# Second layer pair by pair, tiles turned in place, and h and u kept in DRAM tile by tile

## The chip, the cores and the metric

The kernel runs on one core of one Trainium2 chip. The metric is the device time of one execution in microseconds (us). The time outside the profile's span is the execution's own time less the span from its first to its last instruction.

## What is computed

All arrays are float32. The core of the reference:

```python
# attention: batch 4, 12 heads, 448 positions, head size 64
scores = q @ k.T / sqrt(64) - log(448)
x = (sigmoid(scores) @ v), heads side by side           # 1792 x 768
# layer one
h = maximum(maximum(x @ w1, x @ w2), x @ w3)             # 1792 x 768
y = h @ w_out                                            # 768 x 768
# layer two
h = y @ w_in                                             # 1792 x 1024
e = exp(h - max(h))
solu = h * e / sum(e)
ln = (solu - mean(solu)) / sqrt(var(solu) + 1e-6) * g_ln
out = ln @ w_out2                                        # 1024 x 768
```

## The kernel before

**Arithmetic.** Float32 operands are split into a high part and a rest, and each product is three matmuls (high x high, high x rest, rest x high). Layer one and layer two use a Strassen-Winograd scheme: a 2 x 2 block product is seven products P1 to P7 (table `PROD`), on sums and differences of blocks. An operand of a product needs a copy by ScalarE (the high part), a subtraction by VectorE (the rest), and for four of the seven a sum first.

**Stages.** Attention comes first, with the weight conversions between its halves. There the product w_out @ w_in is formed, so that layer two's first half, L, is one product of h with a 768 x 1024 weight. Then layer one runs over 9 column groups times two halves of the batch (`units`). Each unit opens P1, closes P4 and P3 of the unit before, and does P2, P6, P5 and P7. When a block of h is done, `sums` writes it to DRAM (`h_d`). Layer two follows: 14 tiles of 128 rows, taken as seven pairs, first L for all pairs, then O (the product with the last weight). The list `tiles` puts tiles 7 to 13 first, so pair 0 is tiles 7 and 8.

**L and O.** `groups` gives the order: L takes pairs 0 and 1 together, then 2, 3 and 4 alone, then 5 and 6 together; O takes 0 and 1 together and then the others alone. A group opens P1 of its first pair (`begin`), closes P4 and P3 of the group before (`fourth`, `third`), and does P2, P6, P5, P7 (`second`, `sixth`, `fifth`, `seventh`). After P1, P6 and P7 ScalarE copies the PSUM tile X, and the next product of X waits for that copy. An L product is 9 matmuls of 512 columns, an O product 12 of 384. The seven weights of L are loaded by GpSimd (`load_wf`) at the end of layer one; `hold` is a small copy on GpSimd by which its queue waits for a tile. While the last pair of L goes through its products, each product's weight slot is given to a weight of O (`release`, `load_w2`).

**Normalization.** After a pair's P3, `solu_ln` is appended to the queue `lazy`. It is a chain of ScalarE and VectorE steps over two tiles: exponential, product, square, a few small steps on sums, scaling; then VectorE turns 32 x 32 blocks (`dve.transpose`) into an `e` tile and SP writes it to DRAM (`u_d`). `load_u(p)` reads a pair's turned tiles back for O. Its `while` loop writes out steps of the queues until the pair's tiles, and for p > 0 the second tile of pair p + 1, are turned.

**Order.** The queues of TensorE, ScalarE, VectorE and (from the end of layer one) GpSimd run in the order in which the program writes their instructions. Each matmul of layer two adds 0.227 (L) or 0.174 (O) to a budget (`pace`), and steps of `bg` (operands: `prep_l`, `prep_o`) and then of `lazy` are written as long as it is above zero, each taking its cost off. An L pair's operands cost 6.26 together, an O pair's 7.69, a chain of `solu_ln` 6.74, an L sum 0.78, an O sum 0.56. A product whose operand is not yet written out takes steps of `bg` whatever the budget (`product_c`). Operands stand in a ring of 10 slots, one for an L operand and two for an O operand. `load_h` brings a pair's tiles of h from DRAM (`next_h` in layer two).

**Buffers.** L's results and the turned tiles read back share the tag `hu`, 10 buffers (pair 0 has two of its own); `e` has 3.

Of the kernel before, what the change touches and what calls it, by code (L numbers as in the profile page):

```python
# [44 lines left out]
def sigmoid_attention_max_moe_solu_ln(tc, q, k, v, w123, wo, wi, w2, g, out):  # L45
# [56 lines left out]
    h_d = {(k, bp): dram.tile([3, P, 2 * S], F32, name=f"h_d{k}{bp}") for k in range(2) for bp in range(2)}  # L102
# [548 lines left out]
    def sums(u, i, j, ps, add):  # L651
# [20 lines left out]
        if w == 2:  # L672
            sp.dma_start(out=h_d[i, bp][fp, :, j * S : (j + 1) * S], in_=h)
# [26 lines left out]
    def load_h(p, k, rows=slice(0, 3)):  # L700

        for i in range(2):
            bp, c0 = divmod(tiles[2 * p + i] * P, 2 * S)
            sp.dma_start(
                out=h_tile(p, i, k)[:, rows], in_=h_d[k, bp][rows, :, c0 : c0 + P].rearrange("f p t -> p f t")
            )
# [154 lines left out]
    for n, u in enumerate(units):  # L861
# [8 lines left out]
        if old is not None:  # L870
# [4 lines left out]
            if old["u"] == (NG - 1, 1):  # L875
# [7 lines left out]
                for k in range(2):  # L883
                    hold(hts[(1, 1, k)][:, :8])
# [7 lines left out]
        if n == len(units) - 1:  # L892
            bg.append(in_turn(prep_l(0), prep_l(1), 8))
# [5 lines left out]
        if u == (NG - 1, 1):  # L899
# [3 lines left out]
            af_cm, afirst = open_pool("afirst", 1)  # L903
            load_h(0, 0, slice(0, 2))
# [4 lines left out]
            for tag in (0, 1):  # L909
                load_wf(LOADS[tag], tag)  # L910
# [67 lines left out]
    def solu_ln(p):  # L978
# [4 lines left out]
        for i, t in enumerate(pair):  # L983
            e.append(tp.tile([P, 2, 512], F32, tag="e", name=f"e{t}", bufs=3))
# [29 lines left out]
        for i, t in enumerate(pair):  # L1014
            ub = e[i].rearrange("p a b -> p (a b)")
            dve.transpose(out=ub, in_=h[i].rearrange("p a b -> p (a b)"))
            sp.dma_start(out=u_d[t].rearrange("i f r e -> (i f) (r e)"), in_=ub)
            turned.add(t)
            yield 1.25

    def load_u(p):
        for t in tiles[2 * p : 2 * p + 2]:
            while t not in turned or (p + 1 < NP2 and tiles[2 * p + 3] not in turned and p > 0):
                step(bg)
                assert step(lazy), t
            ut = (hfirst if p == 0 else tp).tile([P, 4, 256], F32, tag="hu", name=f"ut{t}", bufs=2 if p == 0 else 10)
            for r in range(4):
                sp.dma_start(out=ut[r * 32 : (r + 1) * 32], in_=u_d[t][:, :, r].rearrange("i f e -> f i e"))
# [28 lines left out]
    def targets(kind, p):  # L1057
# [4 lines left out]
        for t in tiles[2 * p : 2 * p + 2]:  # L1062
            h = (hfirst if p == 0 else tp).tile([P, 2, 512], F32, tag="hu", name=f"h{t}", bufs=2 if p == 0 else 10)
# [98 lines left out]
    groups = [("L", g) for g in ((0, 1), (2,), (3,), (4,), (5, 6))]  # L1162
    groups += [("O", g) for g in ((0, 1), (2,), (3,), (4,), (5,), (6,))]
# [122 lines left out]
```

## Time and profile before

| | |
|---|---|
| median of 3 runs | 701.18 us (698.69 to 705.81) |
| profiled execution, its own time | 700.64 us |
| its span | 698.9 us |
| TensorE busy in the span | 651.9 us, 93% |
| VectorE busy | 490.7 us, 70% |
| ScalarE busy | 372.4 us, 53% |
| mean granted TensorE clock | 0.977 of full speed |

Busy time of TensorE comes from modelled, overlapping matmuls, so a busy TensorE is not one at its peak. A granted clock of 1.00 is 2.4 GHz; the lower level is 1.2 GHz. In the timelines a bracket at the end of a line is the idle time of that engine before the line, and what ended it. Names leave buffer numbers out: `XL` is the PSUM tile X in L, `XO` in O, `c_L_A` and `c_O_S` are operands, `wfB`/`wfT` and `w2tB`/`w2tT` weights, `a` the tiles of h, `ut` the turned tiles.

### The profile page before, as it was taken

The numbers are of one execution on the slowest core, as the hardware profiler recorded it, in microseconds if no ns is written. First come the engines' busy times: TensorE is split into PE (matmuls) and PEld (weight loads), VectorE is DVE, ScalarE is ACT, GpSimd is POOL, SyncE is SP. The second block draws the span as 40 slices with busy tenths as digits, with TensorE's granted clock in tenths as the row PEclk, the third lists the DMA queues.
The fourth block names the chain that finished last, engine by engine and source line by source line (L and its number), as shares of the span: only waits on it lengthen the run. The fifth ranks groups of instructions, "written<-read, shape, count | busy, mean of one in ns | idle before, by whom it ended". The sixth has DMA issues, their size and how long they took to land.

```text
span 698.9 us, 9717 instructions
## 1 busy us (share of the span) xinstructions
PE 651.9 (93%) x3283; PEld 526.4 (75%) x3283; DVE 490.7 (70%) x1070; ACT 372.4 (53%) x712; POOL 72.4 (10%) x149
## 2 busy tenths in 40 slices
PE   9999999999999999999999998899997887786797
PEld 6555688545569999999999997678875786776697
DVE  4799987797458788868977875447885674645552
ACT  5888433678665554554455443235766354635241
POOL 1111110001000111011011001210013500000000
PEclk9999999999999999999999999999999799988999
DMA  8788678736301565654674439992539956362211
GB/s 295 216 257 248 191 270 307 282 122 206 117 1 28 158 193 187 185 153 149 179 218 149 117 110 315 318 364 79 159 91 312 303 167 166 80 181 102 74 46 68
DMA packets 82977, 125.16 MB, mean 179 GB/s; under 512 B 35568, under 2 KB 62704, under 8 KB 82928
## 3 DMA queue, kind: packets, MB, share of 16 engines
q1 hardware_dynamic: 71344, 70.84, 32.5%
q0 software_dynamic: 11440, 53.48, 24.1%
q8 instruction: 26, 0.43, 0.3%
q10 hardware_dynamic: 144, 0.23, 0.1%
q14 instruction: 23, 0.19, 0.1%
HBM read 84.15 MB, written 40.37 MB: 178 GB/s over the span
## 4 chain that ended last, share of the span: by engine, by line
PE 56%; DVE 21%; DMA 8%; ACT 8%; issue 6%; SPq 1%; POOL 0%; DVEq 0%; ACTq 0%; POOLq 0%
PE x L643 18%; PE v L643 9%; PE XO L948 6%; PE z L643 4%; PE av L272 4%; PE XL L948 3%; PE VO L948 3%; PE sc L251 3%; DMA ut<-u_d 2%; PE ZO L948 2%; DMA a<-h_d 2%; ACT e L996 2%; DMA wfT<-w_dT 1%; DVE y_wi L157 1%; ACT h L1012 1%
## 5 line engine op out<-in xcount | busy, mean ns | idle before, releaser
L272 PE MATMUL av<-sf,vr 128*64 128x448 f32 x384 | 77.5, 546 | 0.0
L259 ACT ACTIVATE sf<-sc,bias_s 128x896 f32<-128x896 f32 x72 | 67.6, 1009 | 1.3
L141 POOL DMA_DIRECT2D raw<-in_w x52 | 28.2, 542 | 279.7 <-DVE S L56 140.0
L272 PEld LDWEIGHTS av<-sf,vr 128*64 128x64 f32 x384 | 25.4, 137 | 40.8 <-issue 35.7
L251 PE MATMUL sc<-qt,kt 64*128 64x448 f32 x432 | 52.0, 377 | 3.2 <-ACT sf L256 3.2
L472 PE MATMUL pw<-wi_t,r_wo 128*128 128x512 f32 x216 | 49.6, 391 | 0.0
L251 PEld LDWEIGHTS sc<-qt,kt 64*128 64x128 f32 x432 | 38.2, 185 | 15.1 <-issue 5.9
L472 PEld LDWEIGHTS pw<-wi_t,r_wo 128*128 128x128 f32 x216 | 40.4, 188 | 9.4 <-issue 1.0
L683 ACT COPY u<-x 128x448 f32<-128x448 f32 x36 | 19.1, 530 | 43.2 <-PE x L643 43.2
L948 PE MATMUL XO<-w2tT,c_O_S 128*128 128x384 f32 x168 | 32.4, 340 | 6.6 <-ACT c_O_S L51 6.2
L948 PE MATMUL XL<-wfT,c_L_S 128*128 128x512 f32 x126 | 32.4, 409 | 4.0 <-DMA wfT<-w_dT 3.0
L948 PEld LDWEIGHTS XO<-w2tT,c_O_S 128*128 128x128 f32 x168 | 29.0, 188 | 8.5 <-ACT c_O_S L51 7.2
L643 PE MATMUL x<-T3h,S 128*128 128x448 f32 x108 | 33.7, 366 | 0.0
L643 PE MATMUL x<-B11h,A 128*128 128x448 f32 x108 | 33.7, 366 | 0.0
L643 PE MATMUL x<-T4h,A 128*128 128x448 f32 x108 | 33.6, 365 | 0.0
L643 PE MATMUL x<-T2h,S 128*128 128x448 f32 x108 | 33.6, 365 | 0.0
L643 PE MATMUL v<-B22h,S 128*128 128x448 f32 x108 | 33.6, 365 | 0.0
L643 PE MATMUL z<-B21h,A 128*128 128x448 f32 x108 | 33.6, 365 | 0.0
L643 PE MATMUL v<-T1h,S 128*128 128x448 f32 x108 | 33.6, 365 | 0.0
L948 PEld LDWEIGHTS XL<-wfT,c_L_S 128*128 128x128 f32 x126 | 24.6, 197 | 10.6 <-issue 3.8
L412 ACT ACTIVATE raw<-raw,g_sb 128x192 f32<-128x192 f32 x32 | 13.3, 466 | 31.3 <-DVE raw L157 31.3
L157 DVE SCALAR_TENSOR_TENSOR raw<-raw 128x384 int32<-128x384 int32 x52 | 29.0, 557 | 1.1
(185 smaller groups left out, 1561.6 us busy)
## 6 DMA issues: line engine op xcount, KB each, us to landing
raw<-in_w POOLq DMA_DIRECT2D x52, 384.0 KB, 4.1
w_d<-w2s SPq DMA_DIRECT2D x48, 192.0 KB, 2.4
u_d<-e SPq DMA_DIRECT2D x14, 512.0 KB, 3.0
ut<-u_d SPq DMA_DIRECT2D x56, 128.0 KB, 3.9
kr<-in_k SPq DMA_DIRECT2D x24, 256.0 KB, 3.4
vr<-in_v SPq DMA_DIRECT2D x24, 256.0 KB, 4.0
raw<-in_wi POOLq DMA_DIRECT2D x16, 384.0 KB, 4.5
w_dT<-wsT SPq DMA_DIRECT2D x12, 512.0 KB, 3.5
```

The lines of the kernel that those rows point to most:

```text
L141: pool.dma_start(out=t, in_=source(key).rearrange("p (n t) -> p n t", t=2))
L157: dve.scalar_tensor_tensor(out=yi, in0=raws[key][:, cols, 0], scalar=29, in1=yi, op0=ALU.logical_shift_right, op1=ALU.bitwise_or)
L251: pe.matmul(sc[:, j, :S], lhsT=kt[rows, x, c * P : (c + 1) * P], rhs=qt[rows, y], start=start, stop=stop)
L259: act.activation(sf, sc[:, :, :S], AF.Sigmoid, bias=bias_s, scale=1.0 / math.sqrt(D))
L272: pe.matmul(pa[j * D : (j + 1) * D, :S], lhsT=vr[:, j, c], rhs=sf if c == 3 else sf[:, j], start=(n == 0), stop=(n == 3),)
L412: act.activation(half, half, AF.Copy, scale=g_sb[:, kc + 4 * i : kc + 4 * i + 1])
L472: pe.matmul(ps, lhsT=wt[:, a, cols], rhs=wi_t[:, b, c0 : c0 + 512], start=(i == 0), stop=(i == 3 * KC - 1))
L643: pe.matmul(ps, lhsT=l, rhs=r, start=(start and c == 0 and i == 0), stop=(stop and c == 2 and i == 2), skip_group_check=True)
L683: act.copy(e, ps)
L948: pe.matmul(ps, lhsT=hl[l][:, c * P : (c + 1) * P], rhs=wt[:, c, m], start=(start and c == 0 and i == 0), stop=(stop and c == chunks - 1 a ...
L996: act.activation(e[i], h[i], AF.Square, bias=su[:, c], scale=-float(F2), accum_out=vs[:, c])
L1012: act.activation(h[i], h[i], AF.Identity, bias=nb[:, c], scale=s1[:, c])
```

## The change

- The turn writes back into the h tile (`h[i]`), and the write to DRAM reads from there. `e` has 2 buffers instead of 3, `hu` 11 instead of 10.
- `u_d` is laid out so that a tile is read back by one DMA of whole rows; it is written by four DMAs, one for every 32 partitions, in pieces of 256 words.
- `load_u` waits for its own pair's tiles alone.
- L takes its seven pairs one by one; O is grouped as before. `load_u(2)` and `load_u(3)` come one step later in O's first group, and `next_h(p + 2)` follows P6 of pair p throughout.
- `h_d` holds tiles of 128 rows of h whole, so that `load_h` reads rows of 256 or 384 words in one piece; `sums` writes each block in two DMAs, one with three tiles' columns (128 each) and one with the 64 columns of the tile that two blocks share.
- The first weight of L is asked for before pair 0's tiles of h; the `hold` for pair 1's tiles is gone. Pair 1's operands are queued in pair 0's L group instead of in turn with pair 0's.

```diff
--- before.py
+++ after.py
@@ -99,7 +99,7 @@
 
     w_d = {nm: dram.tile([P, 3, 2 * 512 + 16], F32, name=f"w_d{nm}") for nm in LOADS}
     w2_d = [dram.tile([4, P, len(nms), 2, HU], F32, name=f"w2_d{n}") for n, nms in enumerate(PIECES)]
-    h_d = {(k, bp): dram.tile([3, P, 2 * S], F32, name=f"h_d{k}{bp}") for k in range(2) for bp in range(2)}
+    h_d = {(k, bp): dram.tile([TT // 2, P, 3, P], F32, name=f"h_d{k}{bp}") for k in range(2) for bp in range(2)}
     u_d = [dram.tile([4, 32, 4, 256], F32, name=f"u_d{t}") for t in range(TT)]
 
 
@@ -670,7 +670,12 @@
             tt(add, ps, add, ALU.add)
             tt(h, add, h, ALU.max)
         if w == 2:
-            sp.dma_start(out=h_d[i, bp][fp, :, j * S : (j + 1) * S], in_=h)
+            to, c = h_d[i, bp][:, :, fp], j * D
+            sp.dma_start(
+                out=to[4 * j : 4 * j + 3].rearrange("t p c -> p t c"),
+                in_=h[:, c : c + 3 * P].rearrange("p (t c) -> p t c", t=3),
+            )
+            sp.dma_start(out=to[3, :, c : c + D], in_=h[:, 3 * P * (1 - j) :][:, :D])
 
     def held(u, nm, ps):
         k = state["e"] % 5
@@ -700,10 +705,8 @@
     def load_h(p, k, rows=slice(0, 3)):
 
         for i in range(2):
-            bp, c0 = divmod(tiles[2 * p + i] * P, 2 * S)
-            sp.dma_start(
-                out=h_tile(p, i, k)[:, rows], in_=h_d[k, bp][rows, :, c0 : c0 + P].rearrange("f p t -> p f t")
-            )
+            bp, t = divmod(tiles[2 * p + i], TT // 2)
+            sp.dma_start(out=h_tile(p, i, k)[:, rows], in_=h_d[k, bp][t][:, rows])
 
     def last_rows(k):
 
@@ -880,8 +883,6 @@
                 last_rows(1)
                 for k in range(2):
                     load_h(1, k)
-                for k in range(2):
-                    hold(hts[(1, 1, k)][:, :8])
                 for tag in (2, 3, 4):
                     load_wf(LOADS[tag], tag)
         Z = ps_z.tile([P, 512], F32, tag="z", name=f"z{n}")[:, :S]
@@ -890,7 +891,7 @@
         product(X, u, "P6", False, False)
         u2 = held(u, "u2", X)
         if n == len(units) - 1:
-            bg.append(in_turn(prep_l(0), prep_l(1), 8))
+            bg.append(prep_l(0))
         V = ps_v.tile([P, 512], F32, tag="v", name=f"v{n}")[:, :S]
         product(V, u, "P5", True, False)
         product(X, u, "P7", False, False)
@@ -901,13 +902,13 @@
             shut(xd_cm)
             wslot.update(weight_slots("sa", (0, 1)))
             af_cm, afirst = open_pool("afirst", 1)
+            load_wf(LOADS[0], 0)
             load_h(0, 0, slice(0, 2))
             load_h(0, 1, slice(0, 2))
             for k in range(2):
                 hold(hts[(0, 1, k)][:, :8])
             last_rows(0)
-            for tag in (0, 1):
-                load_wf(LOADS[tag], tag)
+            load_wf(LOADS[1], 1)
         old = dict(u=u, X=X, V=V, u2=u2)
     assert not raws and state["load"] == len(stream)
 
@@ -981,7 +982,7 @@
         h = [h2s.pop(t) for t in pair]
         e = []
         for i, t in enumerate(pair):
-            e.append(tp.tile([P, 2, 512], F32, tag="e", name=f"e{t}", bufs=3))
+            e.append(tp.tile([P, 2, 512], F32, tag="e", name=f"e{t}", bufs=2))
             c = slice(i, i + 1)
             act.activation(e[i], h[i], AF.Exp, bias=low[:, c], scale=-1.0, accum_out=ssum[:, c])
             yield 0.05
@@ -1012,20 +1013,23 @@
             act.activation(h[i], h[i], AF.Identity, bias=nb[:, c], scale=s1[:, c])
             yield 0.05
         for i, t in enumerate(pair):
-            ub = e[i].rearrange("p a b -> p (a b)")
-            dve.transpose(out=ub, in_=h[i].rearrange("p a b -> p (a b)"))
-            sp.dma_start(out=u_d[t].rearrange("i f r e -> (i f) (r e)"), in_=ub)
+            ub = h[i].rearrange("p a b -> p (a b)")
+            dve.transpose(out=ub, in_=ub)
+            for r in range(4):
+                sp.dma_start(
+                    out=u_d[t][:, :, r].rearrange("b f e -> f b e"),
+                    in_=ub[r * 32 : (r + 1) * 32].rearrange("f (b e) -> f b e", b=4),
+                )
             turned.add(t)
             yield 1.25
 
     def load_u(p):
         for t in tiles[2 * p : 2 * p + 2]:
-            while t not in turned or (p + 1 < NP2 and tiles[2 * p + 3] not in turned and p > 0):
+            while t not in turned:
                 step(bg)
                 assert step(lazy), t
-            ut = (hfirst if p == 0 else tp).tile([P, 4, 256], F32, tag="hu", name=f"ut{t}", bufs=2 if p == 0 else 10)
-            for r in range(4):
-                sp.dma_start(out=ut[r * 32 : (r + 1) * 32], in_=u_d[t][:, :, r].rearrange("i f e -> f i e"))
+            ut = (hfirst if p == 0 else tp).tile([P, 4, 256], F32, tag="hu", name=f"ut{t}", bufs=2 if p == 0 else 11)
+            sp.dma_start(out=ut, in_=u_d[t].rearrange("b f i e -> (b f) i e"))
             uts[t] = ut.rearrange("p i (k t) -> p k i t", k=K2)
 
     def prep_o(p):
@@ -1060,7 +1064,7 @@
             return [block(f"{nm}{p}") for nm in ("e1", "u2", "u3", "cx")]
         hh = []
         for t in tiles[2 * p : 2 * p + 2]:
-            h = (hfirst if p == 0 else tp).tile([P, 2, 512], F32, tag="hu", name=f"h{t}", bufs=2 if p == 0 else 10)
+            h = (hfirst if p == 0 else tp).tile([P, 2, 512], F32, tag="hu", name=f"h{t}", bufs=2 if p == 0 else 11)
             h2s[t] = h
             hh.append(h)
         return [hh[0][:, 0], hh[0][:, 1], hh[1][:, 1], hh[1][:, 0]]
@@ -1159,10 +1163,10 @@
         for k in range(2):
             load_h(p, k)
 
-    groups = [("L", g) for g in ((0, 1), (2,), (3,), (4,), (5, 6))]
-    groups += [("O", g) for g in ((0, 1), (2,), (3,), (4,), (5,), (6,))]
+    groups = [("L", (p,)) for p in range(NP2)] + [("O", g) for g in [(0, 1)] + [(p,) for p in range(2, NP2)]]
     prev = None
     for n, (kind, g) in enumerate(groups):
+        p, last = g[-1], n == len(groups) - 1
         if prev and len(prev) > 1:
             for o in prev:
                 fourth(o)
@@ -1184,40 +1188,31 @@
         now_open += [begin(kind, p) for p in g[1:]]
         if n == 2:
             load_w2(LOADS[0], 7)
-        if (kind, g) == ("L", (5, 6)):
+        if (kind, p) == ("L", NP2 - 1):
             load_u(1)
-        elif (kind, g) == ("O", (0, 1)):
-            load_u(2)
-        elif kind == "L" and 2 <= g[0] < 5:
-            next_h(g[0] + 1)
-        last = n == len(groups) - 1
         if not last:
             for o in now_open:
                 second(o)
+        if (kind, p) == ("O", 1):
+            load_u(2)
         for o in now_open:
             sixth(o)
-        if (kind, g) == ("L", (0, 1)):
-            next_h(2)
-        elif (kind, g) == ("L", (4,)):
-            next_h(6)
-            load_u(0)
-            bg.append(in_turn(prep_l(5), prep_l(6), 6))
-        elif kind == "L" and g[0] < 4:
-            bg.append(prep_l(g[0] + 1))
-        elif (kind, g) == ("L", (5, 6)):
-            bg.append(in_turn(prep_o(0), prep_o(1), 1))
+        if kind == "L":
+            if p + 2 < NP2:
+                next_h(p + 2)
+            if p == NP2 - 2:
+                load_u(0)
+            bg.append(prep_l(p + 1) if p + 1 < NP2 else in_turn(prep_o(0), prep_o(1), 1))
         elif not last:
-            bg.append(prep_o(g[-1] + 1))
-            if 2 <= g[0] < 5:
-                load_u(g[0] + 2)
+            bg.append(prep_o(p + 1))
+            if 1 < p < NP2 - 2:
+                load_u(p + 2)
         for o in now_open:
             fifth(o)
-        if (kind, g) == ("L", (0, 1)):
-            bg.append(prep_l(2))
-        elif (kind, g) == ("O", (0, 1)):
-            load_u(3)
         for o in now_open:
             seventh(o)
+        if (kind, p) == ("O", 1):
+            load_u(3)
         if last:
             for o in now_open:
                 second(o)
```

## Rows read from the trace of the kernel before

**Rows 1.** Page, part 2: TensorE busy share and granted clock.

```profile
PE   9999999999999999999999998899997887786797
...
PEclk9999999999999999999999999999999799988999
```

**Rows 2.** Stretches of layer two, cut between products: busy us per engine, clock, DMA.

```profile
429.50:472.80 43.30, 37.08 (x154) 29.75 (x154) 20.94 (x47) 14.99 (x29) 6.96 (x12) 0.96 0.94 342
472.80:487.30 14.50, 14.50 (x65) 11.87 (x64) 11.18 (x25) 8.54 (x19) 0.00 (x0) 1.00 0.29 83
...
517.70:555.00 37.30, 32.08 (x130) 25.83 (x128) 22.27 (x50) 19.47 (x39) 18.06 (x44) 0.91 0.87 275
555.00:596.20 41.20, 33.02 (x169) 30.45 (x170) 26.23 (x51) 20.39 (x38) 1.33 (x4) 0.96 0.60 174
596.20:617.80 21.60, 16.71 (x85) 16.39 (x84) 12.07 (x24) 13.06 (x24) 0.00 (x0) 0.84 0.46 135
617.80:644.10 26.30, 19.35 (x86) 17.27 (x86) 13.67 (x27) 13.14 (x25) 0.00 (x0) 0.87 0.39 113
644.10:668.00 23.90, 17.31 (x86) 15.72 (x85) 12.63 (x22) 7.11 (x15) 0.00 (x0) 0.93 0.27 74
668.00:682.60 14.60, 14.60 (x86) 14.60 (x85) 9.41 (x16) 6.37 (x13) 0.00 (x0) 1.00 0.14 54
```

**Rows 3.** Timeline of TensorE: start, length, work, idle before and its releaser.

```profile
429.30 0.37 PE L643 MATMUL x<-T3h,S 128*128 128x448 f32 x1
432.86 2.31 PE L948 MATMUL XL<-wfB,c_L_A 128*128 128x512 f32 x9 [3.19 <-DMA wfB<-w_dB]
...
541.60 7.14 PE L948 MATMUL XL<-wfT,c_L_A 128*128 128x512 f32 x18 [5.18 <-ACT h L1148]
...
550.68 4.28 PE L948 MATMUL VL<-wfB,c_L_S 128*128 128x512 f32 x18
...
611.63 4.21 PE L948 MATMUL XO<-w2tT,c_O_A 128*128 128x384 f32 x12 [4.89 <-ACT u L1148]
...
692.96 2.27 PE L948 MATMUL VO<-w2tB,c_O_S 128*128 128x384 f32 x12
```

**Rows 4.** Timeline of ScalarE around two late copies.

```profile
539.84 1.15 ACT L986 ACTIVATE e<-h,st 128x1024 f32<-128x1024 f32 x1 [5.18 <-DMA u_d<-e]
...
604.60 1.15 ACT L996 ACTIVATE e<-h,st 128x1024 f32<-128x1024 f32 x1 [0.81 <-DVE h L990]
...
608.85 2.37 ACT L1012 ACTIVATE h<-h,st 128x1024 f32<-128x1024 f32 x2 [1.02 <-DVE st L1008]
611.12 0.46 ACT L1148 COPY u<-XO 128x384 f32<-128x384 f32 x1
```

**Rows 5.** Timeline of GpSimd where the seven weights are asked for.

```profile
424.54 1.53 POOL L735 DMA_DIRECT2D wfB<-w_dB  x2 [0.66 <-DMA h_d<-hs]
...
439.28 0.58 POOL L731 COPY gate<-a 128x8 f32<-128x8 f32 x1 [1.88 <-DMA a<-h_d]
439.88 1.52 POOL L735 DMA_DIRECT2D wfT<-w_dT  x2
447.97 0.76 POOL L735 DMA_DIRECT2D wfT<-w_dT  x1 [6.57 <-issue]
```

**Rows 6.** Groups of VectorE instructions, layer two: busy us, mean ns, idle before.

```profile
L1016 DVE STREAM_TRANSPOSE e<-h 128x1024 f32<-128x1024 f32 x14 | 17.0, 1233 | 7.9 <-ACT h L1012 6.5 <-DMA u_d<-e 1.3
L990 DVE SCALAR_TENSOR_TENSOR h<-h,e 128x1024 f32<-128x1024 f32 x14 | 16.9, 1221 | 0.8 <-ACT e L986 0.8
```

**Rows 7.** DMA issues of the page, part 6: KB each, us to landing.

```profile
w_d<-w2s SPq DMA_DIRECT2D x48, 192.0 KB, 2.4
u_d<-e SPq DMA_DIRECT2D x14, 512.0 KB, 3.0
ut<-u_d SPq DMA_DIRECT2D x56, 128.0 KB, 3.9
```

**Rows 8.** DMA issues from 416 to 450 us, same columns.

```profile
a<-h_d SPq DMA_DIRECT2D x11, 192.0 KB, 10.1
```

## The prediction

> **What bounds the kernel now.** I read the busy shares in slices first, then a table of stretches, then the two timelines that explain the worst stretches. The slices show TensorE at nine tenths or more for the first two thirds of the span, and between six and nine tenths after that, with the granted clock at full speed nearly everywhere but in two later slices [rows 1]. So attention, the weight product and layer one leave nothing to win; layer two (L, then O) does. The stretches say how much. One L pair alone takes 14.5 us for seven products, 2.07 us each; one undisturbed O pair takes 14.6 us, 2.09 us each, both with TensorE busy throughout and the clock at 1.00 [rows 2]. Against these two prices I read three segments of the profiled execution (span 698.9 us, its own time 700.64 us, so 1.74 us lie outside the span; the median of the runs, 701.18, is the same within 0.1%):
> - Start: from the end of layer one's fifth product of the last unit, 429.7 us, to 472.8 us, 43.1 us for 15 L products and two leftovers of layer one. TensorE waits 3.19 us for the first weight, and later weights trail [rows 3, 5].
> - L: 472.8 to 555.0 us (end of the last V product of pairs 5 and 6), 82.2 us for 34 L products and one O product, which need 34 x 2.07 + 2.09 = 72.5. Excess 9.7 us. The table and the timeline put almost all of it late: a 5.18 us wait for a copy by ScalarE and 18 products behind it at the low clock, 7.14 us instead of 4.1 [rows 2, 3].
> - O: 555.0 to 695.2 us, 140.2 us for 48 O products, which need 48 x 2.09 = 100.3. Excess 39.9 us: four stretches of 41.2, 21.6, 26.3 and 23.9 us stand where 14, 7, 7 and 7 products need 29.3, 14.6, 14.6 and 14.6, so 11.9, 7.0, 11.7 and 9.3 us [rows 2]. The last two pairs have none.
>
> What ends those waits is not a busy engine: in the O stretches VectorE is busy 52 to 64% and ScalarE 30 to 61% [rows 2]. It is order. The load of a pair's turned tiles (load_u) may be written only when the *next* pair's second tile is turned, and until then it writes the next pair's whole normalization chain, at once, into the pinned queues of ScalarE and VectorE. Seen at pair 2 of O: the chain runs on ScalarE from the squares at 604.60 to the scaling that ends at 611.2, with pauses for VectorE inside; the copy that frees X stands behind it, at 611.12; TensorE waits 4.89 us for it and then does 12 matmuls in 4.21 us, the pace of the lower level of its clock, 1.2 instead of 2.4 GHz [rows 3, 4]. The forced chain also drives the budget below zero by its whole cost (6.74), so the next pair's operands come only when a product demands them: the excess goes on in the following stretches, the fourth of which holds no chain at all.
>
> **The change, part by part.**
>
> *Own pair alone (the condition in load_u), and single L pairs.* I follow the budget by hand. An L pair earns 63 x 0.227 = 14.3; its four sums take 3.1 and the next pair's operands 6.26, so 4.9 is left for a chain of 6.74. Chain 0 is ready at the end of pair 0, starts in pair 1, and with 4.9 a pair chains 0 to 3 are written out by pair 6's second product. From pair 6's fifth product to the sixth of O's pair 2, the place where pair 4 is asked for, 4 L products of 2.04 and 17 O products of 2.09 earn 43.7; sums take 6.2, the operands of O's pairs 0 and 1 15.4 and most of pair 2's about 7. Some 15 are left, or 2.2 chains: 4 and 5 are out when pair 4 is asked for, and 6 before pair 5 is. So no load forces a chain, and operands fall behind by one step (at most 1.32) instead of a whole chain. What remains are chains written at the budget's pace, of which O carries three (4, 5, 6) instead of about four. A pair with a chain fits: VectorE's 9.41 us plus (17.0 + 16.9) / 7 = 4.8 us, ScalarE's 6.37 us plus 6 calls, 7.0 us, each under 14.6 us [rows 2, 4, 6], though barely. A chain can still stand before a copy. The cost per chain is bounded by what the trace shows: nothing (the stretch 472.8 to 487.3 carries most of chain 0 and has no wait [rows 2]) and 7.0 us (the wait and the slow products above). I take 2 us each, near the lower end since the pace is that of the lower row, and 2 us for the doubled first group: O's excess 8 (3 to 25), a gain of 32. For L, 3 (1 to 8) instead of 9.7.
>
> *Turning in place, two e tiles, eleven hu tiles.* The turn itself keeps its 1.24 us [rows 6]. The wait that goes is the one in front of ScalarE's exponential at 539.84, 5.18 us for the write of an e tile still under way [rows 4]; that is the L wait named above, and its 6.7 us gain is counted there. What is late next: an hu tile. Eleven make the second turned tile of pair p take the place of the next pair's first h tile, so this load still waits for that tile's write. SP stands there, and behind it in its queue the output writes; nobody waits for either for a pair's time. I cost it at 0; without that cover it costs the write and load, 3.0 + 3.9 us, once a pair [rows 7].
>
> *Turned tiles written in four and read in one.* Both versions issue 14 x 5 DMAs; the write takes the form of the old reads (3.9 us), the read that of the old write (3.0 us) [rows 7]. Sum 0, and hidden, as each load has nearly a pair's lead.
>
> *h in DRAM by tiles.* 24 more small writes on SP, which is idle there, and loads of whole rows of 1,024 or 1,536 bytes instead of 512. Between 416 and 450 us such loads take 10.1 us beside the weights [rows 8]; the larger rows can only help. I cost it at 0 (0 to -2). The Trainium skill, "DMA: Bandwidth & Descriptors", section "Specifications", speaks against the 64-column rows: it says that writes under 512 bytes are done as read-modify-write. Here the w_d writes go in pieces of 96 columns, 384 bytes, and land in 2.4 us, sooner than the turned tiles' 1 KB pieces [rows 7]. If each new small write did cost such a time again, only the last before pair 1's load would count, and the sum would be 664 instead of 662.
>
> *Weights at the start.* The first is asked for when layer one has left its slot, at about 417 us instead of 424.5, and the gate that held the third until 439.9 is gone [rows 5]. But one pair now eats all seven weights. Seven times 1.57 MB (128 x 3 x 1,024 words), the tiles of pairs 0 to 2 (2.1 MB) and layer one's last h (1.4 MB) are 14.5 MB; at 342 to 400 GB/s, the first being the mean of that stretch [rows 2], 36 to 42 us from 417.5: the seventh lands at 454 to 460. It is needed by the last product of pair 0, and six more follow before the mark: 456 + 2.1 + 6 x 2.07 + some low clock = 472. The same as before: the 3.19 us won at the first weight are paid back at the fourth to seventh. I take 0, bounds -3 and +7 (the first weight no earlier than now).
>
> Sum: 700.6 + 0 - 6.7 - 32 = 662 us.
>
> **Rivals.**
> - *Chains go on costing.* Paced or not, a chain's 6.6 us on ScalarE stands before a copy that has one product of cover. If each of O's three still costs the 7.0 us of pair 2, O's excess is 23 with the first group's 2: 677. For it: both engines are then over 90% full. Against: chain 0's stretch.
> - *The change doesn't remove the wait.* Eleven tiles against twelve still tie pair p's load to pair p + 1's chain; if that holds back the operands as now, O's 39.9 stay and only L's 6.7 go: 694, no measurable change beside 700.6 (a difference under 1% can't be told from none in this kernel). Against: only ScalarE's and VectorE's written order made the wait, and the tile's turn is already in it.
> - *Slower.* Singles leave only one product, 2.07 us, between the third X copy and the product that needs X; in the old first and last groups there were two or more. If each of the seven chains is written just ahead of that copy, each costs what the pairs with 7.0 and 11.7 us lost, on average 9.4, so 66 us instead of the 9 in my sum (3 + 8, less the first group's 2): 662 + 57 = 719. It decides against the change once a chain costs over 7 us on average. Against: the L singles of now, with no wait between 472.8 and 487.3 [rows 2].
>
> **How the numbers follow.** Forecast 0.68, its own range 650 to 677 from start -3 to +7, L 1 to 5, O 3 to 14. Chains go on costing: 0.17. Wait not removed: 0.08. Slower: 0.07. Low end: 662 - 3 - 2 - 5 - 2 = 650. High end: into the first rival with the start's +7 and part of its O bound: 677 + 9 = 686. That leaves out the last two, 0.15. Faster by over 1% are the first two, 0.85; within 1% the third; slower the fourth.
>
> **What would show it.** Right: TensorE's waits for the third copies gone or under 2 us; no wait of the exponential for a DMA; four O stretches within 2 us of their products; all but three chains before O; the low clock in fewer slices. The start should show waits for the fourth to seventh weight. Wrong, if chains still run in unbroken blocks ahead of copies, if TensorE waits for operands in O as now, or if pair 1's operands wait for h tiles behind the weights.

## The result and the profile after

| | before | after |
|---|---|---|
| median of 4 runs each | 702.15 us (698.69 to 705.81) | 663.30 us (660.67 to 665.47) |
| ratio, 95% interval | | 0.944 (0.938 to 0.951) |
| profiled execution, its own time | 700.64 us | 665.47 us |
| its span | 698.9 us | 663.7 us |
| TensorE busy | 93% | 97% |
| mean granted TensorE clock | 0.977 | 0.994 |

The kernel is 5.6% faster; 662 us was forecast. In the slices of the page after (tenths of busy time; granted clock), the run of sevens and eights that ended the kernel before [rows 1] is gone, and what is left of it lies at the start of layer two, in slices 27 and 28:

```profile
PE   9999999989999999999999999967999999999897
...
PEclk9999999999999999999999999997999999999999
```

The same three segments as in the prediction, by the same marks (S from the end of layer one's fifth product of the last unit to pair 2's P2, L from there to the end of the last V product, O to the last matmul):

| segment | before | after | its products need | predicted |
|---|---|---|---|---|
| S | 43.1 | 49.3 | | 43 |
| L | 82.1 | 74.7 | 72.5 | 75.5 |
| O | 140.3 | 102.4 | 100.3 | 108.3 |

The table of stretches of the kernel after answers [rows 2]. Its columns are busy time of TensorE, weight load, VectorE, ScalarE and GpSimd, then clock, DMA share, GB/s. First S, then L, then O cut at its pairs:

```profile
433.70:483.00 49.30, 38.87 (x155) 30.25 (x154) 24.18 (x51) 18.85 (x39) 5.89 (x10) 0.93 0.81 302
483.00:557.70 74.70, 73.19 (x321) 59.41 (x320) 62.83 (x143) 49.41 (x93) 10.26 (x25) 1.00 0.53 164
557.70:587.00 29.30, 29.20 (x168) 28.88 (x167) 22.11 (x42) 19.63 (x38) 8.99 (x23) 1.00 0.93 326
587.00:601.60 14.60, 14.60 (x86) 14.60 (x85) 10.80 (x24) 9.39 (x19) 0.00 (x0) 1.00 0.34 122
601.60:616.20 14.60, 14.60 (x86) 14.60 (x85) 12.61 (x20) 9.26 (x19) 0.00 (x0) 1.00 0.71 211
616.20:632.80 16.60, 14.91 (x86) 14.59 (x85) 10.43 (x24) 8.88 (x17) 0.00 (x0) 1.00 0.26 72
```

O's four bad stretches of before, 41.2, 21.6, 26.3 and 23.9 us, are 29.3, 14.6, 14.6 and 16.6. VectorE and ScalarE do the same work in both kernels (490.7 and 372.4 us busy before, 491.2 and 372.5 after); only its place changed. The timeline of TensorE after (its columns as in [rows 3]) shows where waits remain:

```profile
442.06 2.35 PE L949 MATMUL ZL<-wfB,c_L_A 128*128 128x512 f32 x9 [2.48 <-DMA wfB<-w_dB]
447.33 3.63 PE L949 MATMUL XL<-wfT,c_L_S 128*128 128x512 f32 x9 [2.92 <-DMA wfT<-w_dT]
452.67 2.34 PE L949 MATMUL VL<-wfT,c_L_S 128*128 128x512 f32 x9 [1.71 <-DMA wfT<-w_dT]
457.24 3.34 PE L949 MATMUL XL<-wfT,c_L_S 128*128 128x512 f32 x9 [2.23 <-DMA wfT<-w_dT]
...
466.37 2.31 PE L949 MATMUL VL<-wfB,c_L_S 128*128 128x512 f32 x9 [1.10 <-DMA wfB<-w_dB]
...
490.27 2.34 PE L949 MATMUL XL<-wfT,c_L_S 128*128 128x512 f32 x9 [0.94 <-ACT h L1141]
...
628.52 2.35 PE L949 MATMUL XO<-w2tT,c_O_A 128*128 128x384 f32 x12 [1.69 <-ACT u L1152]
```

Five waits for weights in S, 10.4 us together, where before had 3.19, 2.77 and 0.26; then three waits of 0.45 to 1.69 us to the end, 3.1 together. The two products of 3.63 and 3.34 us behind such waits ran partly at the lower clock: the granted clock of these two stretches is 0.59 and 0.66.

The own times of the two profiled executions differ by 35.2 us. S gives +6.2, L -7.4, O -37.9, and layer one +4.1, together -35.0 (the rest lies behind the last matmul): in this execution of the changed kernel layer one ends at 433.7 us instead of 429.7. That last term is not the change's (last section).

### The profile page after: what moved, and what is told of

Read it like the earlier page. It is cut to its first block, busy times and chain, and to the rows that moved or that the text cites. A ratio compares the mean times of both kernels' runs of the same rounds, so it can differ in the third digit from the quotient of the medians.

```text
span 663.7 us, 9697 instructions
## 1 busy us (share of the span) xinstructions
PE 641.9 (97%) x3283; PEld 518.2 (78%) x3283; DVE 491.2 (74%) x1070; ACT 372.5 (56%) x712; POOL 72.0 (11%) x147
## 4 chain that ended last, share of the span: by engine, by line
PE 62%; DVE 18%; DMA 7%; ACT 7%; issue 5%; SPq 0%; POOL 0%; ACTq 0%; DVEq 0%
PE x L643 19%; PE v L643 9%; PE XO L949 7%; PE z L643 5%; PE av L272 5%; PE XL L949 4%; PE VO L949 3%; DMA h_d<-hs 3%; PE sc L251 3%; PE VL L949 2%; PE ZO L949 2%; ACT e L997 2%; DVE y_wi L157 1%; DMA wfB<-w_dB 1%; DMA a<-h_d 1%
## 5 line engine op out<-in xcount | busy, mean ns | idle before, releaser
L251 PEld LDWEIGHTS sc<-qt,kt 64*128 64x128 f32 x432 | 38.4, 184 | 15.1 <-issue 5.9
L949 PE MATMUL XL<-wfT,c_L_S 128*128 128x512 f32 x126 | 33.9, 417 | 6.2 <-DMA wfT<-w_dT 5.1
L949 PEld LDWEIGHTS XO<-w2tT,c_O_S 128*128 128x128 f32 x168 | 29.3, 188 | 0.0
```

The costliest lines, as they stand in the source:

```text
L251: pe.matmul(sc[:, j, :S], lhsT=kt[rows, x, c * P : (c + 1) * P], rhs=qt[rows, y], start=start, stop=stop)
L949: pe.matmul(ps, lhsT=hl[l][:, c * P : (c + 1) * P], rhs=wt[:, c, m], start=(start and c == 0 and i == 0), stop=(stop and c == chunks - 1 a ...
```

## The experiments

The table has all runs: the segments of the profiled execution, the median of four runs, and the ratio to the kernel before on the same chip. Those medians of before lie between 697.6 and 702.2 us, so ratios of different rows compare to about half a per cent. Segments come from one execution each; L and O compare well, S less so (52.0 in e1, with the start of after).

| kernel | S | L | O | median us | ratio (95%) |
|---|---|---|---|---|---|
| before | 43.1 | 82.1 | 140.3 | 702.15 | |
| after | 49.3 | 74.7 | 102.4 | 663.30 | 0.944 (0.938 to 0.951) |
| a1_old_condition | 48.3 | 74.7 | 104.6 | 665.04 | 0.948 (0.942 to 0.954) |
| b1_own_pair_alone | 42.4 | 83.8 | 128.8 | 688.78 | 0.981 (0.976 to 0.986) |
| s1_singles_alone | 53.9 | 83.6 | 104.5 | 677.98 | 0.965 (0.960 to 0.970) |
| e1_turn_into_e | 52.0 | 88.4 | 104.5 | 683.48 | 0.977 (0.973 to 0.982) |
| a3_old_first_loads | 51.6 | 74.8 | 102.4 | 664.12 | 0.952 (0.950 to 0.955) |
| a4_old_h_layout | 51.0 | 74.7 | 102.4 | 663.87 | 0.953 (0.949 to 0.956) |
| a5_old_u_layout | 48.7 | 74.8 | 105.3 | 663.77 | 0.950 (0.945 to 0.955) |
| a2_first_two_together | 39.1 | 74.6 | 112.4 | 660.65 | 0.941 (0.936 to 0.945) |
| c1_faster_budget | 39.2 | 84.4 | 100.5 | 658.86 | 0.943 (0.941 to 0.946) |
| c2_later_asks | 38.6 | 74.6 | 118.7 | 666.60 | 0.955 (0.952 to 0.958) |
| d1_o_budget | 38.4 | 74.6 | 105.4 | 653.85 | 0.936 (0.930 to 0.941) |
| d2_both_budgets | 38.5 | 76.1 | 102.4 | 654.35 | 0.936 (0.931 to 0.941) |

**The condition in load_u.** Once put back into the changed kernel, once changed alone with what it needs (the turn in place and its buffers), L grouped as before:

```diff
 a1, against after:
-            while t not in turned:
+            while t not in turned or (p + 1 < NP2 and tiles[2 * p + 3] not in turned and p > 0):
 b1, against before: that line the other way, the turn in the h tile, e 2, hu 11, and
-            bg.append(in_turn(prep_o(0), prep_o(1), 1))
+            bg.append(in_step([prep_o(0), prep_o(1)]))
```

(`in_step` takes one step of each in strict alternation, so that b1 is not the condition alone.)

> The changed kernel with one condition put back: the load of a pair's turned tiles again asks for the next pair's second tile. If what pays is that no load forces a chain (my theory), the price follows from how far the chains are written when the loads ask: chains 0 to 4 are out in time, 5 half, 6 not begun, so one and a half of the seven chains are forced at 7 us each and operands fall behind as before: 672 to 682 us, with the late third copies back at the pairs 2 and 3 of O only. If the condition alone made the old excess of O, it is back at 690 or more. If the single pairs of L did it all, nothing changes: 661 to 667.

> The kernel before with the turn in place, two e tiles, eleven hu tiles and the load that asks for its own pair alone; L and O grouped as before, h and u laid out as before, weights asked for as before (the operands of O's first two pairs strictly by turns, which the order of the ring needs here). My theory: the budget has written three and a half chains at the start of O and each later one before it is asked for, so most of the excess of O (39.9 us) and of late L (9.7) goes, while the start stays at its 43 us: 660 to 672 us. If the single pairs are what pays: 692 to 702.

Put back, the condition costs 2.2 us of O, and 1.7 us between medians that were not taken side by side. My own theory had 672 to 682 us and missed; 665.0 lies where the single pairs do it all. One copy is late, by the mechanism that I named (a whole chain, then the copy behind it): TensorE of a1

```profile
610.02 2.35 PE L949 MATMUL XO<-w2tT,c_O_A 128*128 128x384 f32 x12 [2.63 <-ACT u L1152]
```

Changed alone, it takes 11.5 us off O and leaves 28.5 us of excess; 688.8 us lies in neither of the ranges that I gave. In b1 chains 4, 5 and 6 reach their turns 43, 62 and 86 us after the end of L (before: 26, 55 and 82; after: 21, 45 and 69), and chains that come so late are forced by the load of their own pair instead of the pair ahead. TensorE, then ScalarE of b1:

```profile
619.47 4.21 PE L961 MATMUL XO<-w2tT,c_O_A 128*128 128x384 f32 x12 [4.25 <-ACT u L1161]
```

```profile
544.11 0.59 ACT L1161 COPY h<-XL 128x512 f32<-128x512 f32 x1 [6.88 <-DMA u_d<-h]
...
616.68 2.37 ACT L1025 ACTIVATE h<-h,st 128x1024 f32<-128x1024 f32 x2 [1.02 <-DVE st L1021]
618.96 0.45 ACT L1161 COPY u<-XO 128x384 f32<-128x384 f32 x1
```

The first of ScalarE's lines is b1's 83.8 us in L: a turn in place moves the wait for the write from the e tile to the hu tile, and with two pairs open at once (L's pairs 5 and 6) a new h tile is wanted before the write has landed.

**Single L pairs alone.** Before, with the loops of the new `groups` and the loads that move with them, everything else old:

```diff
-    groups = [("L", g) for g in ((0, 1), (2,), (3,), (4,), (5, 6))]
-    groups += [("O", g) for g in ((0, 1), (2,), (3,), (4,), (5,), (6,))]
+    groups = [("L", (p,)) for p in range(NP2)] + [("O", g) for g in [(0, 1)] + [(p,) for p in range(2, NP2)]]
...
```

> The kernel before with L's pairs one by one and the loads placed as in the changed kernel; old condition, old e and hu tiles, old layouts, old order of the first loads. My theory: chains are written earlier than in the kernel before, but the last two are still forced and the exponential can still wait for the write of an e tile: 672 to 688 us. If the single pairs did it all: 661 to 667. If only the condition counts: 695 or more.

O is 104.5 us with the old condition and the old turn: 35.8 of the 37.9 us that O won come with this edit alone. Chains 0 to 3 are turned before L ends (before: 0 to 2). It has a price at both other segments. S grows by 10.8: one pair takes all seven weights in turn, and TensorE stands for them. L does not gain, since the exponential still waits for a write. TensorE, then ScalarE of s1:

```profile
433.18 2.30 PE L948 MATMUL XL<-wfB,c_L_A 128*128 128x512 f32 x9 [3.30 <-DMA wfB<-w_dB]
448.35 4.04 PE L948 MATMUL XL<-wfT,c_L_S 128*128 128x512 f32 x9 [7.15 <-DMA wfT<-w_dT]
...
556.62 4.21 PE L948 MATMUL XL<-wfT,c_L_S 128*128 128x512 f32 x9 [5.01 <-ACT h L1137]
```

```profile
554.86 1.15 ACT L986 ACTIVATE e<-h,st 128x1024 f32<-128x1024 f32 x1 [4.79 <-DMA u_d<-e]
```

**The turn in place.** a1 with the turn into an e tile again; the two differ in this alone:

```diff
-            ub = h[i].rearrange("p a b -> p (a b)")
-            dve.transpose(out=ub, in_=ub)
+            ub = e[i].rearrange("p a b -> p (a b)")
+            dve.transpose(out=ub, in_=h[i].rearrange("p a b -> p (a b)"))
...
 e 3 buffers, hu 10
```

> The changed kernel with the old condition in load_u and with the turn written into an e tile again (three e tiles, ten hu tiles); single L pairs and everything else stay as changed. It is compared with a1, which differs from it in the turn and its buffers alone. Theory (the exponential waits for the write of an e tile that was turned into): L goes from 74.7 to 82 to 84 us, ScalarE waits for DMA u_d<-e before exponentials in L, O stays within 4 us of a1's 104.6; median 672 to 677. Rival (the L excess of the singles-alone kernel, 83.6 us, came from the old layouts of h and u, not from the turn): L stays at 75 to 77, median 664 to 667.

More than expected: L 88.4 against 74.7, median 18.4 us over a1's. ScalarE waits three times for the write of an e tile; twice the copy of X behind the exponential is so late that TensorE stands for it, and then works at the lower clock. ScalarE, then TensorE of e1:

```profile
493.77 1.15 ACT L987 ACTIVATE e<-h,st 128x1024 f32<-128x1024 f32 x1 [2.36 <-DMA u_d<-e]
...
537.97 1.15 ACT L987 ACTIVATE e<-h,st 128x1024 f32<-128x1024 f32 x1 [3.11 <-DMA u_d<-e]
...
561.77 1.15 ACT L987 ACTIVATE e<-h,st 128x1024 f32<-128x1024 f32 x1 [7.90 <-DMA u_d<-e]
...
562.92 0.56 ACT L1141 COPY h<-XL 128x512 f32<-128x512 f32 x1
```

```profile
495.54 3.54 PE L949 MATMUL XL<-wfT,c_L_S 128*128 128x512 f32 x9 [3.42 <-ACT h L1141]
563.54 4.21 PE L949 MATMUL XL<-wfT,c_L_S 128*128 128x512 f32 x9 [8.35 <-ACT h L1141]
```

The two waits, less the 0.95 that a1 has, are 10.8 us, and the slow products behind them 3.1 (3.54 + 4.21 instead of 2 x 2.34): the 13.7 us of L within 0.2. After has the same group of exponentials with no DMA among its releasers, though its writes are the same; groups of VectorE and ScalarE from 430 us on, columns as in [rows 6]:

```profile
L1017 DVE STREAM_TRANSPOSE h<-h 128x1024 f32<-128x1024 f32 x14 | 17.3, 1240 | 7.3 <-ACT h L1013 7.3
...
L987 ACT ACTIVATE e<-h,st 128x1024 f32<-128x1024 f32 x14 | 16.0, 1144 | 6.5 <-DVE st L974 6.5
```

S is 3.7 us longer as well in e1, with a wait of 3.40 us for the seventh weight. The first turn of e1 starts at 488.25 us, behind the end of S at 485.75, so the turn itself can't be the reason; what is was not found.

**The start and the layouts.** Three kernels undo one part of the change each:

```diff
 a3:
+                for k in range(2):
+                    hold(hts[(1, 1, k)][:, :8])
...
-            load_wf(LOADS[0], 0)
             load_h(0, 0, slice(0, 2))
...
-            load_wf(LOADS[1], 1)
+            for tag in (0, 1):
+                load_wf(LOADS[tag], tag)
 a4:
-    h_d = {(k, bp): dram.tile([TT // 2, P, 3, P], F32, ...
+    h_d = {(k, bp): dram.tile([3, P, 2 * S], F32, ...
 a5 (one write, four reads):
+            sp.dma_start(out=u_d[t].rearrange("i f r e -> (i f) (r e)"), in_=ub)
...
+            for r in range(4):
+                sp.dma_start(out=ut[r * 32 : (r + 1) * 32], in_=u_d[t][:, :, r].rearrange("i f e -> f i e"))
```

> The changed kernel with the old order of the first loads: pair 0's tiles of h before the first weight, and the gate for pair 1's tiles before the third. Singles alone, with old layouts and old loads, had a start of 53.9 us; the changed kernel has 48 to 49. If the order of the first loads makes that difference, the start is 53 to 55 us here and the time 667 to 671 us; if the layout of h makes it, the start stays at 48 to 50 us and the time at 661 to 666.

> The changed kernel with h in DRAM as before: one write of 448 columns, loads of 128 columns at a time. If the layout helps the loads beside the weights, the start grows from 48 to 49 us to 51 to 54; if its small writes, which land late and stand in front of other loads in SP's queue, cost more than the larger rows win, it shrinks to 45 to 48; if neither counts, the time is that of the changed kernel, 661 to 666 us.

> The changed kernel with the old layout of the turned tiles in DRAM (one write of a tile, four reads) and everything else as changed. Theory (both forms issue five DMAs a tile and neither stands on the path): S 48 to 51, L 74.7, O 102 to 104, median 661 to 666, no difference. Rival (the one read of whole rows is what lets a pair's turned tiles land in time, or the shorter write frees the h tile sooner): O or L grows by 3 us or more, median over 668.

L and O do not answer to the first two. S is 51.6 and 51.0 against the 48.3 to 49.3 of after, a1 and a5, but e1, with the new start and layouts, has 52.0, so neither difference is clear of that spread (I had expected 53 to 55 or 48 to 50 for a3, and 51 to 54 for a4 if the layout helps). The start of the seventh weight's product, counted from the end of layer one, says more: 35.1 us in a3, against 31.7 to 33.8 in after, a1, a5 and e1, and 32.6 in a4. So the old order of the first loads is late by a little more than the spread, and the old layout of h is not late at all: a4's longer S lies mostly in that product itself, 3.88 us instead of 2.3, at a granted clock of 0.56. On the medians, which are within 1 us of a5's in the same range of ratios, neither can be told from nothing. With pairs 0 and 1 together the two changes show better, though not one by one: S is 38.4 to 39.2 in the five kernels that have them (a2, c1, c2, d1, d2) and 43.1 and 42.4 in before and b1. The layout of the turned tiles makes no difference to the median (663.77); its O of 105.3 has four waits of 0.5 to 1.7 us, one of them for a weight.

**Grouping and budget.** a2 takes L's first two pairs together again, as before, and O's first two pairs' operands in strict alternation; all else as after. c1, d1 and d2 change the budget per matmul of a2, c2 asks for the tiles of pair p + 2 after P7 instead of P6:

```diff
-    groups = [("L", (p,)) for p in range(NP2)] + [("O", g) for g in [(0, 1)] + [(p,) for p in range(2, NP2)]]
+    groups = [("L", (0, 1))] + [("L", (p,)) for p in range(2, NP2)] + [("O", g) for g in [(0, 1)] + [(p,) for p in range(2, NP2)]]
...
-        chunks, dt = (3, 0.227) if kind == "L" else (4, 0.174)
+        chunks, dt = (3, 0.25) if kind == "L" else (4, 0.174)    # c1
+        chunks, dt = (3, 0.227) if kind == "L" else (4, 0.19)    # d1
+        chunks, dt = (3, 0.235) if kind == "L" else (4, 0.185)   # d2
```

> The changed kernel with L's pairs 0 and 1 together again, the rest of L one by one (operands of pairs 0 and 1 in turn as before; those of O's first two strictly by turns). If the start grew from 43.1 to 49.1 us because one pair eats seven weights, it is back at 42 to 45 us, and the time is 656 to 662 us, unless the chains, which begin one pair later, cost in O what the start wins. If the start grew by the order of the first loads and the h tiles alone, it stays at 47 to 50 us.

> Pairs 0 and 1 together (as in the run before), and an L matmul earns 0.25 instead of 0.227, one more chain's worth over the five single pairs. There the last chain was forced by its own pair's load and cost O 10 us. If that is a matter of the budget alone, O's excess falls from 12 to 2 to 5 us while L's stays at 2 to 4: 650 to 655 us. If VectorE can't do more in L (it is busy 84% there), L grows by what O wins: 657 to 664.

> Pairs 0 and 1 together, and in O the load of a pair's turned tiles is asked for after P7 instead of after P6 of the pair two before. The budget gains two products, 4.2 of a chain's 6.74. If the last chain is then written mostly in time: O's excess 3 to 8 us instead of 12, time 652 to 657 us. If the asked-for chain still stands before the third copy, only moved by one product: 658 to 662.

> The changed kernel with L's pairs 0 and 1 together and O's first two pairs' operands in strict alternation (as in a2), and O's budget raised from 0.174 to 0.19 for each matmul. In a2 chain 6 was not yet written out when its own pair was asked for and cost 10 us of O. Theory (the chain comes late by about one chain's cost over some 250 matmuls, 6.7 / 250 = 0.027 at most and about half of it suffices): no chain is forced, O's excess falls from 12 to 2 to 5 us, S 39, L 74.6, median 650 to 655. Rival (a faster budget in O puts chain steps ahead of copies as c1 showed for L): O's excess stays at 8 us or more, median 657 to 663.

> As d1, with the two budgets raised by less each: L's from 0.227 to 0.235 and O's from 0.174 to 0.185 for each matmul. Theory (what is wanted is half a chain more by the time pair 6 is asked for; a small rise in each stage gives it without crowding either): L 74.6 to 77, O 102 to 105, S 39, median 650 to 656. Rival (any rise in L puts chain steps ahead of the copies, since L's pairs have no room): L 79 to 85 and the O gain is eaten, median 657 to 663.

a2's S is 39.1, 10 us under after's: two pairs give each weight two products, and the weights land in time. But O loses 10.0 of it. Chain 6 is written as one block where its pair is asked for, and the copy behind it is late; TensorE and ScalarE of a2, the same picture as [rows 3, 4]:

```profile
619.19 4.21 PE L962 MATMUL XO<-w2tT,c_O_A 128*128 128x384 f32 x12 [4.90 <-ACT u L1165]
```

```profile
616.40 2.37 ACT L1026 ACTIVATE h<-h,st 128x1024 f32<-128x1024 f32 x2 [1.02 <-DVE st L1022]
618.68 0.46 ACT L1165 COPY u<-XO 128x384 f32<-128x384 f32 x1
```

c1 lets chains run earlier in L: O then has no excess (100.5), but L has 9.8 us more than a2's, most of it in eight waits of 0.3 to 2.0 us, 8.2 together, all but the first for a late copy. c2 is worse than both of the ranges that I gave: the load's place only moves the forced block in front of another copy (a wait of 6.52 us). d1 and d2 give the few steps that are missing where there is room. Both are 1.4 to 1.5% under a5, which is measured against the same runs of before and is the changed kernel but for a layout that cost nothing in the median. They have the lowest medians of this study, and the two can't be told apart. Stretches of d2, by the three segments:

```profile
429.70:468.20 38.50, 35.41 (x154) 28.37 (x153) 21.08 (x47) 15.00 (x29) 5.55 (x10) 1.00 0.98 370
468.20:544.30 76.10, 73.81 (x321) 59.35 (x320) 62.40 (x142) 51.77 (x101) 10.58 (x26) 1.00 0.54 166
544.30:646.70 102.40, 100.43 (x576) 99.62 (x574) 72.43 (x137) 58.03 (x113) 10.37 (x22) 1.00 0.58 187
```

## Why the prediction was right, and where not

The time was right, and in part by luck: two of its terms were mis-sized by about 6 us each and cancel. From the forecast of 662 to the profiled execution's 665.5: +4.1 layer one, +6.2 S, -0.8 L, -5.9 O. (Two readings in it were off and change no term: the 7.14 us line that I called 18 products at the low clock is 18 matmuls, two products; and three slices of the page before are below full clock, not two.)

**O (predicted excess 8, from 3 to 25; measured 2.1, under the lower bound).** The mechanism held: order, not engine time. The hand count of the budget held as well: chains 0 to 3 are out before L ends (chain 3 turned at 547), and three chains are left to O. Chains 4 and 5 cost nothing there where I took 2 us each. Chain 6 was to be out before pair 5 is asked for and is not: from its squares on it is written where its own pair is asked for, between the copies after P6 and P7. So one load still forces a chain, and it costs the 2.0 us of the stretch at 616.2. ScalarE after:

```profile
625.73 2.37 ACT L1013 ACTIVATE h<-h,st 128x1024 f32<-128x1024 f32 x2 [1.02 <-DVE st L1009]
628.01 0.46 ACT L1152 COPY u<-XO 128x384 f32<-128x384 f32 x1
```

The doubled first group costs 0, not 2. A chain's price was thus at the lower of my two bounds twice in three. The signs that I named for this part came: no third copy is waited for longer than 1.69 us, the O stretches are within 2.0 us of their products, and the low clock shows in one slice of the page, at the start, where before three had it.

What the term got wrong is whose gain it is. I treated "own pair alone" and the single L pairs as one part and argued from the condition. The condition is worth 2 us (a1); the singles carry nearly all of it, even with the old condition (s1), while the condition without the singles leaves 28.5 us (b1). A forced chain costs 2 us with nothing else late behind it (after), about 4 with one late operand behind it (O's whole excess in a1 and s1), and 7 us and more where several operands are late too (before, a2). That the singles help because each chain can start when its own pair ends is what the turn times say, and a2 fits; but in a2 the order of O's operands changed too, and which part of the regrouping (the last two pairs apart, or the two loads one step later) does most was not separated.

**L (predicted excess 3, from 1 to 8; measured 2.2).** Right, with the wait named: the exponential no longer waits for a write. I gave the turn 6.7 us, the loss seen before. With the other edits in place it is worth 13.7 in L (e1). A likely reason is that the singles put a pair's exponentials closer behind the writes of the pair ahead; s1, with the old layouts, has 8.9 us over after's L, and what makes the rest was not separated. The hu tile cost nothing, as costed, with pairs taken singly; with two open at once it costs 5 us (b1).

**The layouts.** u_d 0: right by the median (a5). h_d, for which I gave 0 to -2: no gain is shown by itself (a4), and "SP is idle there" was wrong. The waits of SP from 420 to 470 us have a row that before has not, the second write of a block waiting for another write of h, 5.4 us in three waits; and the landing times of the same stretch show the small write to be the slower (before's tiles of 128 KB, from the same window, last):

```profile
SPq L678 <- DMA h_d<-hs: 5.4, 3, 2.3
```

```profile
a<-h_d SPq DMA_DIRECT2D x4, 128.0 KB, 6.2
h_d<-hs SPq DMA_DIRECT2D x7, 192.0 KB, 7.3
h_d<-hs SPq DMA_DIRECT2D x7, 32.0 KB, 9.7
```

```profile
a<-h_d SPq DMA_DIRECT2D x3, 128.0 KB, 2.7
```

The Trainium skill, "DMA: Bandwidth & Descriptors", section "Specifications", on transfers under 512 bytes, says that these are done as read-modify-write. The 9.7 us of these 256-byte pieces agree with it better than the 2.4 us of [rows 7] that I set against it. But all of these land beside the weights here, and the same 96 KB of w_d, in 384-byte pieces, took 5.5 us after, beside the first weight, and 2.6 before. So what share the rule has is not shown, and no loss by the layout as a whole is.

**S (predicted 0, from -3 to +7; measured +6.2 in this execution, +5.2 and +5.6 in a1 and a5, +8.9 in e1).** Inside the bounds here, but the term was mis-sized, at the landing of the seventh weight. GpSimd after (compare [rows 5]):

```profile
421.57 0.75 POOL L738 DMA_DIRECT2D wfB<-w_dB  x1 [15.35 <-PE x L643]
431.14 0.19 POOL L734 COPY gate<-a 128x8 f32<-128x8 f32 x1 [8.82 <-DMA a<-h_d]
...
432.58 0.79 POOL L738 DMA_DIRECT2D wfB<-w_dB  x1
433.37 0.76 POOL L738 DMA_DIRECT2D wfT<-w_dT  x1
442.32 0.77 POOL L738 DMA_DIRECT2D wfT<-w_dT  x1 [8.19 <-issue]
447.50 0.77 POOL L738 DMA_DIRECT2D wfT<-w_dT  x1 [4.42 <-DMA h_d<-hs]
452.93 0.77 POOL L738 DMA_DIRECT2D wfT<-w_dT  x1 [4.66 <-DMA h_d<-hs]
457.41 0.76 POOL L738 DMA_DIRECT2D wfB<-w_dB  x1 [3.71 <-issue]
```

All times here are 4.1 us later than before's. The first weight is asked for at 417.5 by before's count, as I had it. The seventh is asked for at 457.4 and its product starts at 466.4, 462.3 by before's count, where I had it landing at 454 to 460. From there to the mark nothing waits, so this landing alone sets where S ends. The stretch from the first ask to that product, then its part up to the second ask, then the part from there to the seventh:

```profile
421.57:466.37 44.80, 34.37 (x143) 27.85 (x141) 21.37 (x45) 11.46 (x24) 8.35 (x13) 0.92 1.02 363
421.57:432.58 11.01, 11.01 (x56) 10.21 (x55) 6.32 (x15) 2.35 (x6) 1.53 (x3) 1.00 1.00 297
432.58:457.41 24.83, 15.49 (x62) 11.69 (x61) 12.19 (x24) 7.11 (x14) 3.85 (x5) 0.93 1.02 378
```

The rate held: 363 GB/s, inside my 342 to 400, with the DMA engines busy throughout. The bytes did not: 16.3 MB passed where I had counted 14.5, and the 1.8 MB more are 4.9 us at that rate. Left out were above all tiles of pair 3 and the first weights of O, both asked for before the seventh weight has landed. I had also overlooked the gate for pair 0's tiles, which stays. These tiles now travel beside the first weight and land in 6.2 us instead of 2.7 (7.0 in a4, with the old layout), so the second and third weights go out 11 us after the first. In those 11 us the rate was 297 GB/s; at the later 378 the same bytes take 2.4 us less, which is an estimate of the gate's price. This account is worked out from the trace alone; no run leaves out the gate or the transfers that I had not counted. Five of the seven products wait, the second and third among them, where my sign had the fourth to seventh. By the kernels: the singles cost +10.8 (s1); with the new order of the first loads and h's new layout S is 4.6 to 5.6 us shorter than that in after, a1 and a5, and 1.9 in e1.

**The rivals.** Chains that go on costing 7.0 us each: no, 2.0 for one of three. The wait not removed: no, O's excess is 2.1 instead of 39.9. Slower by chains in front of the third copy: it did not decide here, but it is real, and c1 shows its price: 9.8 us in L as soon as the budget runs 10% faster.

## What to carry to other kernels

Where engines' queues run in written order, a long chain of small steps has to be given out as it becomes available and at the pace that the other work leaves; when something demands it in one block, the price depends on how late everything behind it already is, so change *when the chain becomes available* before changing who demands it. To forecast when a transfer lands, a mean rate served well here; what has to be complete is the list of bytes that move until then, those asked for behind the transfer too, and of the gates ahead of it in its queue. When one part of a change bundles two edits, predict for each with the other left out: the sum here was right and the credit was not.

## What the runs showed of the hardware

Layer one showed two lengths, also where its code is the same (433.7 us in after, 429.7 and 430.0 in a1 and a5). In three of the fourteen profiled executions (after, e1, d1) it ended at 433.7 us, in the others at 429.5 to 430.0, with TensorE busy without a gap and the granted clock 1.00 in both; 214 us of it hold 1037 matmuls in the one and 1057 in the other, 1.9% apart. The same stretch of after and of d2:

```profile
205.00:419.00 214.00, 214.00 (x1037) 194.19 (x1036) 169.41 (x396) 109.58 (x263) 23.23 (x43) 1.00 0.52 146
```

```profile
205.00:419.00 214.00, 214.00 (x1057) 198.09 (x1056) 171.71 (x404) 111.14 (x268) 23.91 (x44) 1.00 0.53 149
```

The four times of the changed kernel, 660.67, 661.19, 665.41 and 665.47 us, fall into two groups about as far apart, though only the last of them has a profile. What sets the pace was not found.

The write of a turned tile, 2.6 to 2.8 us in the median over the whole kernel where it goes in four pieces, took 7.4 us in the median between 550 and 566 us of e1, beside the first weights of O; the wait of 7.90 us lies there. After has the same, 7.5 us between 545 and 566, and nobody waits for it.

Of L's seven weights, 1.57 MB each, GpSimd had two under way at a time: the fourth to seventh are asked for 0.2 to 0.3 us after the weight two ahead of them has landed (442.32, 447.50, 452.93 and 457.41, where the products that waited for those weights start at 442.06, 447.33, 452.67 and 457.24).
